# A fused attention and MLP kernel: a third score buffer for the first four pairs, scores of two row blocks as one step, feed-forward chunks of 512 tokens

## The chip, the cores and the metric

One NeuronCore of a Trainium2 chip runs the whole program. The metric is the time of one execution on the device in microseconds. The core's engines are TensorE (PE in the rows; the loads of its weights are PEld), VectorE (DVE), ScalarE (ACT), GpSimd (POOL) and SyncE (SP), which issues the DMAs.

## What is computed

Four sequences of 576 tokens go through three layers. Blockwise causal attention (8 heads of 64 channels, blocks of 64 tokens); then a layer that turns each channel by an angle and mixes the tokens; then a low-rank token mix and a feed-forward of width 2048:

```python
scores = scale * q @ k^T, masked by block, softmax over keys; x = attn @ v
theta = x @ w_theta
zr, zi = x * np.cos(theta), x * np.sin(theta)
u = x + w_tok_r @ zr + w_tok_i @ zi
x = u + np.maximum(u @ w_ch, 0.0)
u = x + (x^T @ U @ V)^T
out = u + np.maximum(u @ w_ch1, 0.0) @ w_ch2
```

## The kernel before, in words

The work is cut into steps, which are recorded and then put in order by a planner inside the program (class `Line`). It keeps a model of each engine, gives each step a due time (`at_time`, `spread`, and the constants `CFG`), and issues on each engine the ready step with the smallest due time for which buffers are free; a few rounds revise the due times. So the order of each engine is fixed when the program is built, and a change of the buffers (`line.home`) or of the steps moves instructions everywhere. On the chip each engine works its list off in that order and waits where an input is late.

**Attention** works on 16 pairs of heads, four per sequence. For a pair, `prep` loads q, k and v, `smax(gp, t)` makes the softmax of row block t (0 to 4): scores on TensorE into a score buffer `s` of two PSUM banks (one half per head), a memset of the masked corner and a maximum on VectorE, and an exponential with its sum on ScalarE. Blocks 0 and 1 share one score buffer, 0 in its first 128 columns, 1 in columns 256 to 511. There are two score buffers (`ss0`, `ss1`). `norm` divides by the sum, `trans` turns the probabilities over by transposes on TensorE (tiles `t`), and `av` multiplies with v (tiles `oA`, `oB`). While one pair is in `trans` and `av`, the next is in `smax`.

**Mixing**, once per sequence: `theta` (th), `sines` on ScalarE, which loads another table for sines than for exponentials, `product` (transposes xp), `mix_r` and `mix_i` (y), `chan` (c), `lowrank` (xq, G) and `expand` (h). The next sequence's attention runs between.

**Feed-forward**: the 2304 tokens are cut into chunks (`CHUNKS`, line 57). For each of 16 slices f of the width, `ff1` makes 12 matmuls into a tile m, ScalarE and VectorE turn m into hh (its rounded part and the rest), and `ff2` makes 12 matmuls into four accumulators acc. A chunk's input u is read back by `load_u` and split in two parts. The first chunk runs beside the last sequence.

PSUM has eight banks: two for `pa` (t, oA, oB, some others, later acc), two for `pm` (th, xp, y, c, xq, h), four for the two score buffers, which later become a3 and b3 of the feed-forward.

**Fillers.** Where the planner's model has TensorE idle in its first 140 us, `keep_warm` puts transposes of the identity into a bank that is free then:

```python
for i in range(int((o.start - end - 60) / 110)):
    w = Op()
    w.call = [(real.tensor.transpose, (v, ident, ident), {})]
```

In the rows a filler stands under the name of that bank's next tile: th<-ident or t<-ident, with ident alone as its input. Since every instruction is issued by one loop, all have that loop's line.

Of the kernel before, what the change touches and what calls it, by code (L numbers as in the profile page):

```python
# [12 lines left out]
F32 = mybir.dt.float32  # L13
F32R = mybir.dt.float32r
# [10 lines left out]
P = 128  # L25
# [28 lines left out]
NHH = 2  # L54
LOC1 = "BBKKXTTTRRRRRRRB"
LOC2 = "BBKKXTTTTTTKKKKB"
CHUNKS = [512] + [256] * 7
NVV = 2
QW = 640
NPT = 1  # L60
# [119 lines left out]
class Line:  # L180
# [33 lines left out]
    def together(self, way):  # L214

        self.choice = []
        way()
        choice, self.choice = self.choice, None
        o = choice[0]
        o.call = [c for x in choice for c in x.call]  # L220
        o.cost = sum(x.cost for x in choice) + (107.0 if o.mode[0] == 64 else 0.0)
        o.outs, o.ins = [a for x in choice for a in x.outs], [a for x in choice for a in x.ins]
        return self.link([o])

# [303 lines left out]
def build(tc, ctx, qT, kT, v, w_theta, wtokT, w_ch, U, V, w1, w2, outT):  # L528
# [21 lines left out]
    def decode(parts, ta, oh, ol):  # L550
# [12 lines left out]
        if ol is not None:  # L563
# [20 lines left out]
    nc = line = Line(nc)  # L584
    pools = {"wk": ctx.enter_context(tc.tile_pool(name="wk", bufs=1)),
             "ps": ctx.enter_context(tc.tile_pool(name="ps", bufs=1, space=PSUM))}
    ast = ExitStack()
    with tc.using_default_side("right"):
        pools["at"] = ast.enter_context(tc.tile_pool(name="at", bufs=1))
        pools["ps2"] = ast.enter_context(tc.tile_pool(name="ps2", bufs=1, space=PSUM))  # L590
# [3 lines left out]
    for pool, tags in (("wk", {"K": 8, "T": NKT, "R": NR, "RT": NT_, "raw": NRAW, "xT": NXT, "Ust": 1, "Vst": 1}),  # L594
                       ("at", FIRST), ("w1p", THEN)):
        for tag, n in tags.items():
            for i in range(n):
                line.home("ps2" if tag == "ss" else pool, f"{tag}{i}", **{tag: tuple(FIRST) if pool == "w1p" else ()})
    for i in range(2):
        line.home("ps3", f"a3{i}", a3=tuple(FIRST))  # L600
        line.home("ps3", f"b3{i}", hp=tuple(FIRST))
        line.home("ps", f"pm{i}", pm=(), hp=("pm",))
    for i in range(PA):
        line.home("ps", f"pa{i}", pa=())

# [21 lines left out]
    def xtile(name, shape, dt):  # L627
        return line.tile(shape, dt, "xT", name)
# [21 lines left out]
    def smax(gp, t):  # L650
# [5 lines left out]
        nm, sm = x["nm"], x["sm"]  # L656
        q, k = qk[gp]
        if t != 1:
            x["s"] = line.tile([P, 2, 512], F32, "ss", f"s{n}_{t}", PSUM)
        s = x["s"]  # L660
        i = 2 * t
        if t < 4:
            W = P * (t + 1)
            src = s[:, :, 256:512] if t == 1 else s[:, :, :W]
            line.together(lambda: [nc.tensor.matmul(src[:, hh], q[64 * hh:64 * hh + 64, t * P:(t + 1) * P],
                                                    k[64 * hh:64 * hh + 64, :W], start=True, stop=True) for hh in range(2)])
            nc.vector.memset(src[0:64, :, W - 64:W], NEG)
            pt = line.tile([P, 2, W], F32, f"P{t}", f"P{n}_{t}")
            nc.vector.tensor_reduce(out=nm[:, i:i + 2], in_=src, axis=AX.X, op=ALU.max, negate=True)
            for hh in range(2):  # L670
# [344 lines left out]
    def load_u(n):  # L1015
        s0, s1 = starts[n], starts[n + 1]
        w = s1 - s0

        def utile(name, shape):
            return line.tile(shape, F32R, "U", name)  # L1020

        if n == 0:
            us[n] = [utile(f"us{n}_{a}", [P, NC4, w]) for a in range(2)]
        else:
            u = utile(f"us{n}", [P, NC4, 2, w]) if n > 1 else xtile(f"us{n}", [P, NC4, 2, w], F32R)
            us[n] = [u[:, :, a] for a in range(2)]
        uh, ul = us[n]
        for c in range(NC4):
            raw = rawslot(f"u3_{n}_{c}", F32)[:, :s1 - s0]
            for b in range(s0 // S, (s1 + S - 1) // S):  # L1030
                a0, a1 = max(s0, b * S), min(s1, (b + 1) * S)
                nc.sync.dma_start(raw[:, a0 - s0:a1 - s0], u3d[b][c * P:(c + 1) * P, a0 - b * S:a1 - b * S])
            rnd("sh", uh[:, c], raw)
            sub(ul[:, c], raw, uh[:, c], "sl")
# [111 lines left out]
    def place(x):  # L1146
        if not isinstance(x, View):
            return x
        buf = x.buf
        if buf.ap is None:  # L1150
            if buf.home.pool not in pools:
                ast.close()
                with tc.using_default_side("right"):
# [54 lines left out]
```

## Time and profile before

| what | us |
|---|---|
| median of 3 runs (902.42 to 905.83) | 902.61 |
| the profiled execution | 902.81 |
| its span, first to last instruction | 901.0 |
| PE busy | 881.4 |
| DVE busy | 420.6 |
| ACT busy | 393.5 |
| POOL busy | 280.8 |

The profile is of one execution. Its span lies 1.8 us under its time. "Busy" counts an engine's instructions as the profile shows them; TensorE's matmuls overlap, and their ends are modelled, so small waits between them hide in it. Matmuls on 32-bit data (s, oA, oB) stand as two records each in the trace, so a step of two such matmuls is x4 there and x2 in the order.

### The profile page before, as it was taken

Reading aid. Unit: us, or ns where it says so; the run is one execution under the profiler, and the core shown is the slowest. Engines: PE = TensorE matmul, PEld = TensorE weight load, DVE = VectorE, ACT = ScalarE, POOL = GpSimd, SP = SyncE. Lnnn points to the kernel's source line nnn. Section 1 sums busy time; section 2 is a strip of 40 time slices with the busy share of each in tenths; the row PEclk is TensorE's granted clock in tenths of the full one; section 3 lists DMA queues with packets and bytes.
Section 4 is the critical chain, followed back from the end, with each engine's and each line's share of the span. In section 5 each row is a group of like instructions: output and inputs, shape, how many; then the busy total and the mean of one; then the engine's idle time right before and its main releaser. Section 6 shows DMA issues by size and latency. Waiting matters only on the chain.

```text
span 901.0 us, 15779 instructions
## 1 busy us (share of the span) xinstructions
PE 881.4 (98%) x6275; PEld 772.0 (86%) x6275; DVE 420.6 (47%) x855; ACT 393.5 (44%) x932; POOL 280.8 (31%) x334
## 2 busy tenths in 40 slices
PE   8999999998999999999999999999999999999998
PEld 7766688876688787898887978899999999999998
DVE  4876687465644566528957782322121212121211
ACT  5977696469644685545735561121111111111111
POOL 2544455554323532346614533221020202020000
PEclk9999999998999999999999999999999999999999
DMA  5551232011020110124343350130010101000000
GB/s 197 171 157 64 70 108 77 29 42 43 29 95 16 43 43 2 68 105 131 104 135 115 111 179 19 49 99 25 1 46 3 43 6 47 3 25 1 25 1 24
DMA packets 45065, 57.39 MB, mean 64 GB/s; under 512 B 5056, under 2 KB 31168, under 8 KB 44992
## 3 DMA queue, kind: packets, MB, share of 16 engines
q1 hardware_dynamic: 44992, 56.39, 19.4%
q8 instruction: 49, 0.80, 0.4%
q14 instruction: 24, 0.20, 0.1%
HBM read 46.94 MB, written 9.44 MB: 63 GB/s over the span
## 4 chain that ended last, share of the span: by engine, by line
PE 82%; DVE 6%; ACT 6%; DMA 2%; issue 2%; POOL 1%; DVEq 0%; POOLq 0%; ACTq 0%; SPq 0%
PE acc L1162 22%; PE m L1162 22%; PE y L1162 11%; PE th L1162 7%; PE t L1162 5%; PE s L1162 5%; PE c L1162 4%; PE oB L1162 3%; DVE d_w L1162 2%; ACT L1162 1%; ACT P L1162 1%; PE G L1162 1%; PE oA L1162 1%; DMA q<-qT 1%; DVE f L1162 1%
## 5 line engine op out<-in xcount | busy, mean ns | idle before, releaser
L1162 PE MATMUL acc<-hh,w 128*128 128x256 f32 (+1 forms) x1440 | 215.7, 297 | 0.3 <-DVE o L1162 0.2
L1162 PE MATMUL m<-us,w 128*128 128x256 f32 (+1 forms) x1440 | 213.5, 296 | 0.4 <-DVE w L1162 0.4
L1162 PEld LDWEIGHTS acc<-hh,w 128*128 128x128 f32 x1440 | 191.0, 190 | 8.3 <-DVE o L1162 0.8
L1162 PEld LDWEIGHTS m<-us,w 128*128 128x128 f32 x1440 | 189.4, 189 | 7.7 <-DVE w L1162 0.8
L1162 ACT ACTIVATE hh<-m 128x256 fp32r<-128x256 f32 (+1 forms) x128 | 52.5, 410 | 300.6 <-PE m L1162 294.2
L1162 DVE SCALAR_TENSOR_TENSOR hh<-m,hh 128x256 fp32r<-128x256 f32 (+1 forms) x128 | 58.5, 457 | 266.9 <-ACT hh L1162 266.8
L1162 PE MATMUL y<-wtok,zh 128*128 128x288 f32 x576 | 122.6, 303 | 0.2
L1162 PEld LDWEIGHTS y<-wtok,zh 128*128 128x128 f32 x576 | 93.8, 190 | 4.0 <-DVE xT L1162 1.1
L1162 ACT ACTIVATE P<-s,nm 128x128 f32<-128x128 f32 (+2 forms) x144 | 78.7, 550 | 40.8 <-DVE nm L1162 40.5
L1162 PE MATMUL y<-wtok,zl 128*128 128x288 f32 x288 | 86.1, 301 | 0.1
L1162 PE MATMUL t<-ident,P 128*128 128x128 f32 x400 | 65.4, 284 | 5.3 <-DVE PTA L1162 2.5
L1162 PE MATMUL s<-k,q 64*128 64x128 f32 (+4 forms) x320 | 68.5, 467 | 1.8 <-ACT P L1162 1.8
L1162 DVE TENSOR_REDUCE nm<-s 128x2 f32<-128x256 f32 (+4 forms) x80 | 63.7, 805 | 2.4 <-PE s L1162 1.2
L1162 PEld LDWEIGHTS t<-ident,P 128*128 128x128 f32 x400 | 47.1, 143 | 20.3 <-issue 5.2
L1162 PE MATMUL c<-u,wch 128*128 128x288 f32 x384 | 59.1, 301 | 0.9 <-DVE u L1162 0.9
L1162 PEld LDWEIGHTS c<-u,wch 128*128 128x128 f32 x384 | 53.6, 188 | 5.1 <-DVE u L1162 1.3
L1162 PEld LDWEIGHTS y<-wtok,zl 128*128 128x128 f32 x288 | 54.4, 189 | 1.9 <-POOL zl L1162 0.6
L1162 PE MATMUL th<-wth,xh 128*128 128x512 f32 x160 | 51.5, 403 | 0.2
L1162 DVE TENSOR_TENSOR xT<-y,xT 128x288 f32<-128x288 f32 x64 | 28.9, 455 | 47.8 <-PE y L1162 47.3
L1162 POOL TENSOR_SCALAR us<-u 128x256 fp32r<-128x256 f32 x5 | 2.4, 480 | 146.7 <-PE m L1162 73.4
L1162 ACT COPY PTB<-t 128x512 f32<-128x512 f32 (+3 forms) x71 | 30.9, 456 | 37.4 <-PE t L1162 36.0
L1162 POOL TENSOR_TENSOR o<-us 128x256 f32<-128x256 f32 x28 | 20.1, 736 | 85.8 <-DMA outT<-o 84.9
(153 smaller groups left out, 1247.1 us busy)
## 6 DMA issues: line engine op xcount, KB each, us to landing
raw_w<-w SPq DMA_DIRECT2D x32, 512.0 KB, 3.8
raw_tok<-wtokT SPq DMA_DIRECT2D x18, 288.0 KB, 3.0
q<-qT SPq DMA_DIRECT2D x16, 320.0 KB, 2.9
vr<-v SPq DMA_DIRECT2D x16, 320.0 KB, 3.2
k<-kT SPq DMA_DIRECT2D x16, 288.0 KB, 3.4
u3d<-xT SPq DMA_DIRECT2D x16, 288.0 KB, 2.2
outT<-o SPq DMA_DIRECT2D x28, 128.0 KB, 1.8
raw_th<-w_theta SPq DMA_DIRECT2D x8, 256.0 KB, 5.1
```

The costliest lines, as they stand in the source:

```text
L1162: fn(*[place(x) for x in args], **{k: place(x) for k, x in kw.items()})
```

## The change

Four edits. The first four pairs get a third score buffer, `ss2`, in the two banks that `pm` takes over afterwards: `pm` is free only when the last of these buffers (tag `s0`) is done with, and its pool `pp` is opened then. The scores of row blocks 0 and 1 are issued as one step of four matmuls, and both masked corners are filled by one memset of a strided view. The chunks of the feed-forward become 512, 256, 512, 512, 512 tokens; chunk 1 takes its u from one buffer of the tag xT, chunk 3 from two of these, the others from the two large buffers U. And the planner's price of a step of several 64-row matmuls is 53.5 ns per matmul more, where it was 107 per step.

```diff
--- before.py
+++ after.py
@@ -54,7 +54,7 @@
 NHH = 2
 LOC1 = "BBKKXTTTRRRRRRRB"
 LOC2 = "BBKKXTTTTTTKKKKB"
-CHUNKS = [512] + [256] * 7
+CHUNKS = [512, 256, 512, 512, 512]
 NVV = 2
 QW = 640
 NPT = 1
@@ -218,7 +218,7 @@
         choice, self.choice = self.choice, None
         o = choice[0]
         o.call = [c for x in choice for c in x.call]
-        o.cost = sum(x.cost for x in choice) + (107.0 if o.mode[0] == 64 else 0.0)
+        o.cost = sum(x.cost for x in choice) + (53.5 * len(choice) if o.mode[0] == 64 else 0.0)
         o.outs, o.ins = [a for x in choice for a in x.outs], [a for x in choice for a in x.ins]
         return self.link([o])
 
@@ -584,7 +584,8 @@
     nc = line = Line(nc)
     pools = {"wk": ctx.enter_context(tc.tile_pool(name="wk", bufs=1)),
              "ps": ctx.enter_context(tc.tile_pool(name="ps", bufs=1, space=PSUM))}
-    ast = ExitStack()
+    ast, pst = ExitStack(), ExitStack()
+    pools["px"] = pst.enter_context(tc.tile_pool(name="px", bufs=1, space=PSUM))
     with tc.using_default_side("right"):
         pools["at"] = ast.enter_context(tc.tile_pool(name="at", bufs=1))
         pools["ps2"] = ast.enter_context(tc.tile_pool(name="ps2", bufs=1, space=PSUM))
@@ -595,11 +596,15 @@
                        ("at", FIRST), ("w1p", THEN)):
         for tag, n in tags.items():
             for i in range(n):
-                line.home("ps2" if tag == "ss" else pool, f"{tag}{i}", **{tag: tuple(FIRST) if pool == "w1p" else ()})
+                if tag == "ss":
+                    line.home("ps2", f"ss{i}", ss=(), s0=())
+                else:
+                    line.home(pool, f"{tag}{i}", **{tag: tuple(FIRST) if pool == "w1p" else ()})
+    line.home("px", "ss2", s0=())
     for i in range(2):
         line.home("ps3", f"a3{i}", a3=tuple(FIRST))
         line.home("ps3", f"b3{i}", hp=tuple(FIRST))
-        line.home("ps", f"pm{i}", pm=(), hp=("pm",))
+        line.home("pp", f"pm{i}", pm=("s0",), hp=("s0", "pm"))
     for i in range(PA):
         line.home("ps", f"pa{i}", pa=())
 
@@ -656,15 +661,22 @@
         nm, sm = x["nm"], x["sm"]
         q, k = qk[gp]
         if t != 1:
-            x["s"] = line.tile([P, 2, 512], F32, "ss", f"s{n}_{t}", PSUM)
+            x["s"] = line.tile([P, 2, 512], F32, "s0" if gp < 4 else "ss", f"s{n}_{t}", PSUM)
         s = x["s"]
         i = 2 * t
         if t < 4:
             W = P * (t + 1)
             src = s[:, :, 256:512] if t == 1 else s[:, :, :W]
-            line.together(lambda: [nc.tensor.matmul(src[:, hh], q[64 * hh:64 * hh + 64, t * P:(t + 1) * P],
-                                                    k[64 * hh:64 * hh + 64, :W], start=True, stop=True) for hh in range(2)])
-            nc.vector.memset(src[0:64, :, W - 64:W], NEG)
+            if t == 0:
+                both = [(s[:, :, :P], 0, P), (s[:, :, 256:512], P, 2 * P)]
+            elif t > 1:
+                both = [(src, t * P, W)]
+            if t != 1:
+                line.together(lambda: [nc.tensor.matmul(y[:, hh], q[64 * hh:64 * hh + 64, c0:c0 + P],
+                                                        k[64 * hh:64 * hh + 64, :w], start=True, stop=True)
+                                       for y, c0, w in both for hh in range(2)])
+                last = s.rearrange("p h (g c) -> p h g c", c=64)[0:64, :, 1::6] if t == 0 else src[0:64, :, W - 64:W]
+                nc.vector.memset(last, NEG)
             pt = line.tile([P, 2, W], F32, f"P{t}", f"P{n}_{t}")
             nc.vector.tensor_reduce(out=nm[:, i:i + 2], in_=src, axis=AX.X, op=ALU.max, negate=True)
             for hh in range(2):
@@ -1019,11 +1031,13 @@
         def utile(name, shape):
             return line.tile(shape, F32R, "U", name)
 
-        if n == 0:
+        if n == 1:
+            u = xtile(f"us{n}", [P, NC4, 2, w], F32R)
+            us[n] = [u[:, :, a] for a in range(2)]
+        elif n % 2:
+            us[n] = [xtile(f"us{n}_{a}", [P, NC4, w], F32R) for a in range(2)]
+        else:
             us[n] = [utile(f"us{n}_{a}", [P, NC4, w]) for a in range(2)]
-        else:
-            u = utile(f"us{n}", [P, NC4, 2, w]) if n > 1 else xtile(f"us{n}", [P, NC4, 2, w], F32R)
-            us[n] = [u[:, :, a] for a in range(2)]
         uh, ul = us[n]
         for c in range(NC4):
             raw = rawslot(f"u3_{n}_{c}", F32)[:, :s1 - s0]
@@ -1148,6 +1162,9 @@
             return x
         buf = x.buf
         if buf.ap is None:
+            if buf.home.pool not in pools and buf.home.pool == "pp":
+                pst.close()
+                pools["pp"] = ctx.enter_context(tc.tile_pool(name="pp", bufs=1, space=PSUM))
             if buf.home.pool not in pools:
                 ast.close()
                 with tc.using_default_side("right"):
```

Since the planner sets the order, the diff does not show what moves. TensorE's list begins, before, with the first pair's scores (s_0_t is row block t of pair 0; 37 fillers precede them):

```order
L1162 MATMUL th_0_112<-ident 128x128 x37
L1162 MATMUL s_0_0_150<-k_0_95,q_0_93 128x128 x2
L1162 MATMUL s_0_2_155<-k_0_95,q_0_93 128x384 x2
L1162 MATMUL th_0_112<-ident 128x128 x10
L1162 MATMUL s_0_0_150<-k_0_95,q_0_93 128x256 x2
L1162 MATMUL th_0_112<-ident 128x128 x25
L1162 MATMUL s_0_3_213<-k_0_95,q_0_93 128x512 x2
L1162 MATMUL th_0_112<-ident 128x128 x15
L1162 MATMUL s_0_4_252<-k_0_95,q_0_93 128x288 x2
L1162 MATMUL th_0_112<-ident 128x128 x16
```

and after the change:

```order
L1179 MATMUL t_0_0_1_115<-ident 128x128 x37
L1179 MATMUL s_0_0_153<-k_0_98,q_0_96 128x128 x2
L1179 MATMUL s_0_0_153<-k_0_98,q_0_96 128x256 x2
L1179 MATMUL s_0_2_160<-k_0_98,q_0_96 128x384 x2
L1179 MATMUL s_0_3_164<-k_0_98,q_0_96 128x512 x2
L1179 MATMUL t_0_0_1_115<-ident 128x128 x22
L1179 MATMUL s_0_4_205<-k_0_98,q_0_96 128x288 x2
L1179 MATMUL t_0_0_1_115<-ident 128x128 x14
L1179 MATMUL s_1_0_246<-k_1_104,q_1_102 128x128 x2
L1179 MATMUL s_1_0_246<-k_1_104,q_1_102 128x256 x2
```

The scores of blocks 0 and 1 now stand together, blocks 2 and 3 follow at once, and the fillers after the first 37 come later. Over the whole program there are 315 fillers before and 180 after; changes between 64-row scores, matmuls of 64 output columns (oA, oB) and full ones are 142 before and 119 after. Ahead of the first sine, ScalarE has 187 instructions before and 190 after, and VectorE, ahead of the first product with a sine, 182 and 203.

ScalarE's list at the sines of the second sequence (f and c are its angles, P a softmax of the third), before:

```order
L1162 ACTIVATE c_3_2478<-c_3_2478,halfpi 128x512
L1162 ACT_TABLE_LOAD
L1162 ACTIVATE P_1_3_2547,sm_1_2383<-s_1_3_2515,nm_1_2371 128x512
L1162 ACT_TABLE_LOAD
L1162 ACTIVATE f_0_2262<-f_0_2262 128x512
L1162 ACT_TABLE_LOAD
L1162 ACTIVATE P_1_3_2547,sm_1_2383<-s_1_3_2515,nm_1_2371 128x512
L1162 ACT_TABLE_LOAD
L1162 ACTIVATE f_1_2283<-f_1_2283 128x512
L1162 ACT_TABLE_LOAD
L1162 ACTIVATE P_1_4_2614,sm_1_2383<-s_1_4_2520,nm_1_2371 128x576
L1162 ACT_TABLE_LOAD
```

and after:

```order
L1179 ACT_TABLE_LOAD
L1179 ACTIVATE f_4_2380<-f_4_2380,tbias,tscale 128x512
L1179 ACTIVATE c_0_2304<-c_0_2304,halfpi 128x512
L1179 ACTIVATE c_1_2316<-c_1_2316,halfpi 128x512
L1179 ACTIVATE c_2_2384<-c_2_2384,halfpi 128x512
L1179 ACTIVATE c_3_2391<-c_3_2391,halfpi 128x512
L1179 ACTIVATE f_0_2138<-f_0_2138 128x512
L1179 ACTIVATE f_1_2168<-f_1_2168 128x512
L1179 ACTIVATE f_2_2253<-f_2_2253 128x512
L1179 ACTIVATE f_3_2302<-f_3_2302 128x512
L1179 COPY PTB_1_2489<-t_1_2_0_2479 128x3x128
```

The sines now stand together; the program holds 14 table loads before and 8 after.

TensorE's list ahead of the first sequence's mixing (y; xp are transposes for the products), before:

```order
L1162 MATMUL oB_1_1397<-PTB_1_1333,vr_1_1047 64x64 x2
L1162 MATMUL s_2_3_1421<-k_2_1015,q_2_1011 128x512 x2
L1162 MATMUL xp_4_1432<-ident,xd_1257 128x128 x4
L1162 MATMUL t_2_0_1_1450<-ident 128x128 x25
L1162 MATMUL xp_1_1476<-ident,xT_440 128x128 x4
L1162 MATMUL t_2_0_1_1450<-ident 128x128 x26
L1162 MATMUL xp_2_1528<-ident,xT_440 128x128 x4
L1162 MATMUL xp_3_1535<-ident,xT_440 128x128 x4
L1162 MATMUL t_2_0_1_1450<-ident 128x128 x7
L1162 MATMUL y_0_0_0_1556<-wtok_480,zh_8_1481 128x288 x2
```

and after:

```order
L1179 MATMUL oB_2_1443<-PTB_2_1393,vr_2_1089 64x64 x2
L1179 MATMUL xp_1_1465<-ident,xT_440 128x128 x4
L1179 MATMUL t_3_0_0_1488<-ident 128x128 x18
L1179 MATMUL xp_2_1507<-ident,xT_440 128x128 x4
L1179 MATMUL xp_3_1516<-ident,xT_440 128x128 x4
L1179 MATMUL t_3_0_1_1530<-ident 128x128 x7
L1179 MATMUL y_0_0_0_1538<-wtok_564,zh_8_1451 128x288 x2
```

Two of three blocks of fillers are gone or shorter, and before the excerpt now stand the transposes and value products of one more pair of the second sequence, the third instead of the second (oB_2 where it was oB_1).

## Rows read from the trace of the kernel before

**Rows 1.** The page, part 1: busy time and share of the span, by engine.
```profile
PE 881.4 (98%) x6275; PEld 772.0 (86%) x6275; DVE 420.6 (47%) x855; ACT 393.5 (44%) x932; POOL 280.8 (31%) x334
```

**Rows 2.** Stretches: length; busy us (instructions) of PE, PEld, DVE, ACT, POOL; clock, DMA, GB/s.
```profile
8.90:78.10 69.20, 66.96 (x501) 48.44 (x500) 53.94 (x120) 58.43 (x173) 28.56 (x33) 1.00 0.47 152
78.10:117.40 39.30, 38.60 (x248) 27.16 (x247) 24.64 (x54) 28.45 (x74) 16.65 (x22) 1.00 0.21 67
124.50:180.50 56.00, 54.13 (x396) 47.71 (x396) 37.36 (x80) 34.22 (x90) 30.30 (x36) 0.97 0.21 66
180.50:229.20 48.70, 44.19 (x248) 32.75 (x246) 28.95 (x59) 39.50 (x79) 23.12 (x31) 0.93 0.13 40
294.60:338.00 43.40, 42.27 (x270) 33.87 (x268) 25.93 (x57) 31.38 (x69) 20.77 (x27) 1.00 0.14 43
```

**Rows 3.** Chain of waits, 0 to 125 us: start, length, what.
```profile
1.36 6.28 PE th L1162 x37
...
51.10 3.65 DMA q<-qT
...
119.69 2.84 PE t L1162 x26
```

**Rows 4.** Timeline of PE, first softmax: start, length, instruction, [idle before, releaser].
```profile
11.03 0.70 PE L1162 MATMUL s<-k,q 64*128 64x256 f32 x4 [1.08 <-ACT P L1162]
```

**Rows 5.** Chain of waits, 0 to 125 us: scores and value products.
```profile
20.18 0.42 PE s L1162 x4
...
22.18 0.84 PE s L1162 x4
...
82.59 1.07 PE s L1162 x8
...
89.59 0.80 PE oA L1162 x8
90.39 2.05 PE oB L1162 x20
```

**Rows 6.** Timeline of ACT, sines of the second sequence.
```profile
207.33 1.28 ACT L1162 ACT_TABLE_LOAD   x1
...
209.35 2.55 ACT L1162 ACTIVATE c<-c,halfpi 128x512 f32<-128x512 f32 x4
211.91 1.28 ACT L1162 ACT_TABLE_LOAD   x1
```

**Rows 7.** Timeline of PE in the same stretch.
```profile
220.83 1.08 PE L1162 MATMUL xp<-ident,xT 128*128 128x128 f32 x4 [2.27 <-DVE f L1162]
```

**Rows 8.** Stretches around the falls of the clock, columns as in rows 2.
```profile
0.00:5.55 5.55, 4.19 (x20) 4.19 (x21) 0.29 (x6) 0.00 (x0) 1.42 (x7) 1.00 0.60 178
142.00:145.50 3.50, 3.50 (x18) 3.47 (x18) 2.16 (x6) 1.95 (x5) 1.27 (x1) 0.51 0.40 102
220.50:227.40 6.90, 5.99 (x21) 3.68 (x21) 2.65 (x8) 6.84 (x10) 4.67 (x8) 0.51 0.00 0
```

**Rows 9.** Chain of waits: groups of the first chunk, and one place in two chunks of 256.
```profile
535.93 2.80 PE m L1162 x12
538.73 2.80 PE acc L1162 x12
...
621.53 2.86 PE acc L1162 x24
...
667.06 2.86 PE acc L1162 x24
```

**Rows 10.** Groups by line and form (VectorE's additions), and DMA issues of outT.
```profile
L1162 DVE TENSOR_TENSOR o<-acc,o 128x256 f32<-128x256 f32 x28 | 10.5, 425 | 5.8 <-PE acc L1162 5.8
...
L1162 DVE TENSOR_TENSOR o<-acc,o 128x512 f32<-128x512 f32 x4 | 2.7, 682 | 0.0
...
outT<-o SPq DMA_DIRECT2D x4, 256.0 KB, 2.0
...
outT<-o SPq DMA_DIRECT2D x4, 128.0 KB, 1.8
```

## The prediction

> **What bounds the kernel now.** I read the page's busy times first, then the stretches between the marks of the program, then the chain of waits and the timelines. The reader is to see in the page that TensorE is busy for 881.4 of 901.0 us [rows 1]: whatever shortens this kernel has to take work or waits off TensorE. But busy is not useful here: some of it is filler transposes that write nothing anyone reads. Ahead of the first mixing matmul, at 124.5 us, the order has 314 of them, 277 beyond the first 37, which wait for the first load anyway. The first two stretches [rows 2], up to the first sine, have VectorE at 53.94 and 24.64 us and ScalarE at 58.43 and 28.45 us out of 69.20 and 39.30, so neither of these is full, and the fillers stand where TensorE would wait for them.
>
> **Fillers.** 26 of them take 2.84 us in the chain, 0.109 us each [rows 3]. Counted over the order, the program holds 315 before and 180 after. 135 fewer at 0.109 are 14.7 us of TensorE's queue. They are no gain by themselves: each one goes because a real instruction is there to issue earlier, and where that one is late, the engine waits in the filler's place. What releases work earlier can be seen in the first softmax [rows 4]: the scores of row block 1 share their buffer with those of block 0 and wait 1.08 us, until ScalarE has read those; with both issued as one step that wait is gone, and with a third buffer the next pair's scores start before this pair's are read. Whether the helpers can follow is the question. Ahead of the first sine the order puts 203 VectorE instructions instead of 182 (more of the next pairs' softmax) and 190 on ScalarE instead of 187. VectorE's mean in the two stretches is 78.6 us over 174 instructions, 0.45 us, so it gets 9.5 us more, about 88; ScalarE three more at some 0.5, about 88.3 instead of 86.9 [rows 2]. From 8.9 us on, both are then busy until 97 us at the least, and the first sine is at 117.4 now. So it comes from 20 us earlier to not at all. The loads move along on SP's queue: q, k and v have two buffers each, so a pair's load still stands behind the scores of two pairs before, and the chain has a wait of 3.65 us for q [rows 3], which earlier scores can only move. I take that TensorE keeps the share it has now, because the fillers of before filled their gaps with little left over (2.24 us idle in 69.20), which says that the waits are about as long as the order assumes. I charge 1.5 us for busier helpers and the loads; the ends are 0 and, if no filler's time comes back, the first rival. The banks of the third buffer come free with the last scores of the fourth pair; by the order the first theta matmul stands some 30 rows behind those, so nothing waits there. The joint memset of blocks 0 and 1 saves VectorE 16 small ones: nothing, since it isn't full.
>
> **Changes of matmul shape.** A visit to the 64-row scores costs more than its columns: block 0 alone takes 0.42 us, block 2 alone 0.84, both in a row 1.07 [rows 5]. Going there and back thus costs 0.19 us, 0.095 a change. By the order there are 142 changes between the three shapes (64 rows, 64 columns, full) before and 119 after: 23 at 0.095 are 2.2 us.
>
> **The sines of the second sequence.** ScalarE's timeline shows table loads of 1.28 us, and sines and exponentials in turn between them [rows 6]; the program has 14 in all. After the change it has 8, one at the start and two per sequence, less one at the end: the nine sine instructions of a sequence then stand together. From 180.5 to 229.2 us TensorE waits 2.27 us in one piece for f [rows 7], and is idle for 48.70 - 44.19 = 4.51 us in all [rows 2]; and its clock is at 0.51, close to the lower of its two levels, from 220.5 to 227.4 us, right behind this wait [rows 8], which wastes half of 6.90, 3.4 us. Together 7.9. The same stretch of the third sequence, which has no such loads, is still idle for 43.40 - 42.27 = 1.1 us [rows 2]. I take 6.5 us; the ends are 0, if the stall only changes its place, and 7.9. What is late next there is the exponential behind the block of sines (four of them take 2.55 us), and TensorE has the mixing of the first sequence to do meanwhile.
>
> **Feed-forward.** Seven chunks of 256 and one of 512 tokens become one of 256 and four of 512. A steady chunk of 256 takes 667.06 - 621.53 = 45.53 us, the distance of the same place in two chunks; a group of twelve 512-column matmuls takes 2.80, so 32 groups take 89.6 [rows 9]. Three times 2 x 45.53 - 89.6 = 1.46 gives 4.4 us. ScalarE's and VectorE's part of a group lies beside TensorE's, as it does in the 512 chunk now, whose groups follow each other every 2.80 us. At a hand-over VectorE has to empty four accumulators, 4 x 0.68 us [rows 10], while TensorE has two groups of the next chunk to do, 5.6 us: nothing; without that cover 2.7 us each time. A 512 chunk's u needs both large buffers, which come free when the chunk two before has ended, and the chunk between gives the loads 45 or 90 us: nothing. The output of the last chunk is larger: the last addition takes 0.68 instead of 0.42 us and the landing 2.0 instead of 1.8 [rows 10]: 0.5 us more, all of it at the end.
>
> **Sum.** -14.7 - 2.2 - 6.5 - 4.4 + 1.5 + 0.5 = -25.8 us. The profiled execution took 902.81 us, 0.2 above the median of the three, 902.61, so I count from either: 877.
>
> **The clock, and a rule on it.** Before 5.55 us TensorE did nothing but fillers; 20 of them took 4.19 us, 0.21 each, twice the 0.109 of later [rows 3, 8] (the 1.00 that the view prints there is not borne out by them). So such transposes alone brought the clock from the lower level to the upper. Taking 135 of them away can therefore have a price. The rows bound it: where the clock fell, it stayed at 0.51 for 3.5 or 6.9 us [rows 8], at a loss of 1.7 to 3.4 us. I take none, since where fillers go, real matmuls stand closer; the other end is the second rival. The Trainium skill ("TensorE: Matmul & The Clock Gate", Part 4 on transposes) says that the full clock does not engage for transposes, which don't count as a busy engine in the same way. By that rule the fillers never held the clock, and taking them away could not lower it: the sum would be the same 877 and the second rival would fall. The rows here speak against the rule.
>
> **Rivals.** *The helpers are full* (0.2). If ScalarE keeps the 80% it has now (86.9 of 108.5 us), its 88.3 us take 110.4, until 119.3 us: the first sine comes no earlier, and waits take the fillers' place. What is left is the work done ahead by then: by the order one more pair's 25 transposes (2.7 us), its value products (0.80 and 2.05) and the scores of blocks 0 to 2 of the pair behind (0.42, 0.70 and 0.84) [rows 4, 5]. That is 7.5, with 6.5 for the sines and 4.4 - 0.5 for the feed-forward: 885. For it: ScalarE is the fullest of the two now. Against it: it waits in between for maxima that come from TensorE's scores. *The clock falls in the first sequence* (0.03). Thinner fillers leave gaps, each is followed by a drop. A drop costs 1.7 to 3.4 us and the wait ahead of it some 1.5 to 2.3 [rows 7]: some 4.5 us each. Six would eat the 25.8 us; eight in 120 us, one a softmax, give 913, slower than before. Against it: between 8.9 and 124.5 us there is not one now [rows 2]. *More of the waits go* (0.15). Idle time of 2.24 + 0.70 + 1.87 us in the first 180 [rows 2] and the drop at 142 us (1.75) [rows 8] would also go, and the 1.5 that I charged: 869. *The new chunks don't run as the first* (0.02): the hand-over without cover costs 4 x 2.7 = 11 us more: 888.
>
> **Numbers.** The forecast (faster, order of waits as now) has 0.6, with 871 to 884 of its own from the ends of the sine term and of the helpers' charge; 877 is its middle. The range of 868 to 889 takes in the full helpers and the vanished waits with the same play, and leaves out the falling clock and the edges. A measurement of this kernel can tell some 0.5%, 4.5 us, from no change. Faster by more than that: 0.6 + 0.2 + 0.15 and a little of the rest, 0.95; the same 0.03; slower 0.02.
>
> **What would show it.** First mixing matmul near 118 us instead of 124.5 (14.7 and a little less for fillers and changes of shape, 1.5 more for the helpers, and 7.5 of work done ahead), with some 5 us idle before it; 8 table loads; no low clock near 220 us; chunks of 512 tokens every 89.6 us; the last addition 0.68 us. It is wrong if the first mixing comes after 123 us, if a table load stands between two sines, or if TensorE waits at a hand-over.

## The result and the profile after

The changed kernel takes 876.52 us in the median (874.64 to 882.76, 4 runs), the kernel before 902.51 beside it: a ratio of 0.972, interval 0.969 to 0.975. The profiled execution took 876.27 us, its span is 874.5. The forecast of 877.0 was met; how it was met is another matter.

The page's busy times of the changed kernel, which answer to [rows 1]:

```profile
PE 851.5 (97%) x4988; PEld 697.2 (80%) x4988; DVE 434.7 (50%) x814; ACT 378.1 (43%) x868; POOL 241.1 (28%) x273
```

TensorE is busy for 29.9 us less and still fills 97% of the span: the time went off its list. Where, the starts of four matmuls show (us from the span's start, from the timelines):

| mark | before | after | stretch before | stretch after |
|---|---|---|---|---|
| first mixing matmul y | 124.5 | 125.2 | 124.5 | 125.2 |
| first G, sequence 1 | 229.2 | 209.1 | 104.7 | 83.9 |
| first h of the last sequence | 581.6 | 561.3 | 352.4 | 352.2 |
| end | 901.0 | 874.5 | 319.4 | 313.2 |

So nothing was gained ahead of the first mixing (+0.7), 20.8 us between it and the first G, 0.2 from there to the last expansion, and 6.2 in the feed-forward behind it: 26.5 in all.

Stretches of the changed kernel, columns as in [rows 2]; the first two end where theta and the sines of sequence 1 begin, as there:

```profile
8.90:73.10 64.20, 59.46 (x433) 39.77 (x429) 54.87 (x123) 56.86 (x170) 27.70 (x35) 1.00 0.52 167
73.10:116.00 42.90, 40.07 (x246) 27.75 (x244) 32.31 (x73) 32.75 (x86) 15.83 (x22) 1.00 0.23 74
125.20:169.30 44.10, 43.59 (x310) 37.91 (x311) 34.88 (x74) 32.21 (x84) 20.76 (x21) 1.00 0.26 77
169.30:209.10 39.80, 39.80 (x260) 32.84 (x258) 24.11 (x49) 26.33 (x57) 17.67 (x24) 1.00 0.11 32
```

Ahead of the first sine TensorE now idles 4.74 + 2.83 us, where it was 2.24 + 0.70 [rows 2]. Behind the first mixing it idles 0.5 us, where it was 1.87 + 4.51, and the low clock of 3.4 and 6.8 us [rows 8], which wastes half of itself, 5.1, is gone. So 11.0 of the 20.8 us are stalls that vanished; the other 9.8 are work that no longer stands in this stretch. Most of it is done ahead, where TensorE had fillers before: between the two marks the trace has 26 records of t, 12 of s, 8 of oA and 20 of oB fewer, and ahead of the first mixing 25, 16, 8 and 20 more. Four xp and four xq have only moved behind the first G.

The stretch up to the first mixing matmul as a whole, before and after, columns as in [rows 2]:

```profile
0.00:124.54 124.54, 120.02 (x848) 88.57 (x849) 85.64 (x194) 94.01 (x260) 52.10 (x66) 1.00 0.39 128
```
```profile
0.00:125.16 125.16, 114.93 (x783) 80.95 (x784) 96.48 (x216) 98.39 (x274) 49.71 (x68) 1.00 0.42 135
```

TensorE is busy there for 5.1 us less and idle for 5.7 us more. What it waits for is in its waits up to the first mixing matmul (us in total, times, longest), after:

```profile
PE t L1179 <- DVE PTB L1179: 2.4, 4, 0.8
PE s L1179 <- ACT P L1179: 1.7, 3, 0.8
...
PE xp L1179 <- DVE f L1179: 1.2, 2, 0.9
PE t L1179 <- ACT PTB L1179: 1.1, 3, 0.4
```

and three rows of the same view before, where all five add up to 4.1 us, against 9.7 in ten rows after:

```profile
PE s L1162 <- ACT P L1162: 1.3, 2, 1.1
PE t L1162 <- ACT PTA L1162: 0.6, 1, 0.6
PE t L1162 <- ACT P L1162: 0.5, 2, 0.3
```

The transposes t now wait for the copies that empty their two banks (PTB), and xp waits for VectorE's products. The wait for ScalarE's P, which the joint step was to remove [rows 4], is no shorter: it has moved from row block 1 to the scores of block 4.

ScalarE's timeline at the sines of sequence 2, which answers to [rows 6]:

```profile
199.15 1.28 ACT L1179 ACT_TABLE_LOAD   x1
200.44 0.82 ACT L1179 ACTIVATE f<-f,tbias,tscale 128x512 f32<-128x512 f32 x1
201.16 2.54 ACT L1179 ACTIVATE c<-c,halfpi 128x512 f32<-128x512 f32 x4
203.61 2.18 ACT L1179 ACTIVATE f<-f 128x512 f32<-128x512 f32 x4
```

All nine sines are done 6.6 us after the table load starts. TensorE's waits in 125.2 to 209.1 us are two rows, where [rows 7] alone had 2.27:

```profile
PE t L1179 <- ACT P L1179: 0.3, 1, 0.3
PE c L1179 <- DVE xT L1179: 0.2, 1, 0.2
```

In the chain of waits, the chunks of 512 follow each other without a wait ([rows 9] had 45.53 us for half as many tokens):

```profile
692.44 5.60 PE m L1179 x24
698.04 2.76 PE acc L1179 x12
700.80 2.75 PE m L1179 x12
...
781.22 5.44 PE m L1179 x24
...
870.45 0.69 DVE o L1179
```

From 692.44 to 781.22 are 88.8 us, from 603.1, where the chunk before begins, 89.3; the last addition takes 0.69 [rows 10].

### The profile page after: what moved, and what is told of

Its sections match the earlier page's. It is cut to its first block, busy times and chain, and to the rows that moved or that the text cites. A ratio compares the mean times of both kernels' runs of the same rounds, so it can differ in the third digit from the quotient of the medians.

```text
span 874.5 us, 12850 instructions
## 1 busy us (share of the span) xinstructions
PE 851.5 (97%) x4988; PEld 697.2 (80%) x4988; DVE 434.7 (50%) x814; ACT 378.1 (43%) x868; POOL 241.1 (28%) x273
## 4 chain that ended last, share of the span: by engine, by line
PE 48%; DVE 3%; DMA 1%; ACT 1%; issue 1%; ACTq 0%; DVEq 0%; SPq 0%
PE acc L1179 22%; PE m L1179 21%; PE y L1179 3%; PE c L1179 1%; DMA raw_w<-w 1%; DVE d_w L1179 1%; DVE o L1179 1%; ACT d_w L1179 1%; PE G L1179 0%; DVE xT L1179 0%; ACT raw_w L1179 0%; PE xq L1179 0%; PE h L1179 0%; DVE w L1179 0%; DVE zl L1179 0%
## 5 line engine op out<-in xcount | busy, mean ns | idle before, releaser
L1179 PE MATMUL acc<-hh,w 128*128 128x512 f32 (+1 forms) x900 | 205.1, 373 | 1.9 <-DVE hh L1179 1.4
L1179 PE MATMUL m<-us,w 128*128 128x512 f32 (+1 forms) x900 | 202.9, 372 | 0.0
L1179 PEld LDWEIGHTS acc<-hh,w 128*128 128x128 f32 x900 | 157.1, 188 | 35.1 <-DVE hh L1179 2.3
L1179 DVE SCALAR_TENSOR_TENSOR hh<-m,hh 128x512 fp32r<-128x512 f32 (+1 forms) x80 | 50.9, 636 | 264.9 <-ACT hh L1179 264.8
L1179 PEld LDWEIGHTS m<-us,w 128*128 128x128 f32 x900 | 156.6, 188 | 30.2
L1179 ACT ACTIVATE hh<-m 128x512 fp32r<-128x512 f32 (+1 forms) x80 | 44.4, 555 | 292.7 <-PE m L1179 287.6
L1179 PE MATMUL s<-k,q 64*128 64x128 f32 (+4 forms) x320 | 65.2, 452 | 1.8 <-ACT P L1179 1.7
L1179 POOL TENSOR_TENSOR o<-us,us 128x512 f32<-128x512 f32 x16 | 22.0, 1404 | 125.0 <-DVE o L1179 84.2
L1179 ACT COPY PTB<-t 128x384 f32<-128x384 f32 (+3 forms) x66 | 29.4, 454 | 33.2 <-PE t L1179 32.0
L1179 ACT ACTIVATE P<-P,rs 128x128 f32<-128x128 f32 (+4 forms) x72 | 38.4, 592 | 4.1 <-DVE rs L1179 4.1
```

Source lines behind the costliest of these rows:

```text
L1179: fn(*[place(x) for x in args], **{k: place(x) for k, x in kw.items()})
```

## The experiments

Twelve kernels, in the order of the questions. "Later" and "earlier" compare profiled executions, times are medians; the kernel before took 902.9 to 903.8 us beside them. The marks are those of one execution each, and they scatter: up to the last sequence e_chunks has TensorE's list of the kernel before and e_attn that of the changed kernel, and their first mixing comes 1.0 us later and 1.9 us earlier than there. A difference of marks under 2 us shows nothing by itself. The times of the changed kernel scatter over 8 us. The marks of all kernels, in us:

| kernel | time | first mixing | first G | between | fillers | table loads |
|---|---|---|---|---|---|---|
| before | 902.5 | 124.5 | 229.2 | 104.7 | 315 | 14 |
| after | 876.5 | 125.2 | 209.1 | 83.9 | 180 | 8 |
| e_chunks | 897.1 | 125.6 | 230.6 | 105.0 | 315 | 14 |
| e_attn | 881.1 | 123.3 | 207.5 | 84.2 | 180 | 8 |
| e_twobuf | 884.9 | 129.4 | 216.0 | 86.6 | 217 | 8 |
| e_nojoint | 894.3 | 121.1 | 222.1 | 101.0 | 257 | 16 |
| e_sines | 901.3 | 124.4 | 226.6 | 102.2 | 315 | 8 |
| e_loads | 886.0 | 125.0 | 215.6 | 90.6 | 180 | 14 |
| e_nofill_after | 880.8 | 126.7 | 211.6 | 84.9 | 0 | 8 |
| e_nofill_before | 905.6 | 126.9 | 230.7 | 103.8 | 0 | 14 |
| e_pe | 880.9 | 129.3 | 213.7 | 84.4 | 257 | 8 |
| e_act | 879.6 | 126.2 | 210.2 | 84.0 | 180 | 8 |
| e_dve | 881.8 | 129.2 | 212.9 | 83.7 | 180 | 8 |
| e_eps | 875.6 | 122.8 | 206.5 | 83.7 | 180 | 8 |

### Which part of the change is worth what

**e_chunks**: the kernel before with the new chunks alone.

```diff
-CHUNKS = [512] + [256] * 7
+CHUNKS = [512, 256, 512, 512, 512]
...
+        if n == 1:
+            u = xtile(f"us{n}", [P, NC4, 2, w], F32R)
...
```

> The kernel before with the new chunks (512, 256, 512, 512, 512) alone; TensorE's list is the same as before up to the end of the last sequence. Theory A (a 512-column group costs 2.80 us against two of 1.423 of 256 columns): 902.5 - 4.4 + 0.5 = 898.6. Rival B (the feed-forward stretch of the changed kernel was 6.2 us shorter than before, and all of that is due to the chunks): 896.3. Between them lies the fall of the clock at 582 us, which before has and the changed kernel has not: if this run has it too, A.

Measured: 897.05 us, ratio 0.993 (0.991 to 0.996), 6.3 us: between A and B, nearer B. The fall of the clock at 582 us isn't in this profile. From the start of the third chunk (the second of 256, or of 512) to the end it takes 270.9 us, where the kernel before takes 276.8; the clock stayed up in this stretch in both while TensorE worked.

**e_attn**: the changed kernel with the old chunks, the same edit undone.

> The changed kernel with the old chunks (512 and seven of 256); third buffer and joint step stay, TensorE's list is the changed kernel's up to the end of the last sequence. Theory A: the chunks are worth 4 us also here, so 876.5 + 4 = 880.5, and the attention part alone gives 22 us of the 26. Rival B: with the old chunks the hand-overs or the loads of u disturb the last sequence, and the two parts don't add up: over 884.

Measured: 881.07 us, ratio 0.977 (0.975 to 0.979). The attention part alone gives some 22 us; 4.6 of the 26 are missing, the feed-forward's. The same stretch to the end takes 276.8 us here and 271.4 in the changed kernel. Theory A holds: the two halves of the change add up within what the medians tell apart (22.3 + 6.3, against 26.0 to 27.3).

**e_twobuf**: the changed kernel without the third buffer.

```diff
-    line.home("px", "ss2", s0=())
```

> The changed kernel without the third score buffer; joint step and new chunks stay. Its order has 217 fillers (180 in the changed kernel, 315 before) and 8 table loads. Theory A (before the first mixing ScalarE and VectorE set the time, so what TensorE could start earlier is worth little there): 876 to 880, with the first mixing at 124 to 128 us. Rival B (the prediction's own account: 37 more fillers are 37 x 0.109 = 4.0 us of TensorE's queue): 880.5. Rival C (the third buffer is what brings most of the gain): over 888.

Measured: 884.89 us, ratio 0.980 (0.978 to 0.983), 8.4 us over the changed kernel by the medians, 7.9 by the spans, between what B and C expected. 4.2 us come ahead of the first mixing matmul, 2.7 between it and the first G.

**e_nojoint**: the changed kernel without the joint step.

```diff
-            if t == 0:
-                both = [(s[:, :, :P], 0, P), (s[:, :, 256:512], P, 2 * P)]
...
+            line.together(lambda: [nc.tensor.matmul(src[:, hh], q[64 * hh:64 * hh + 64, t * P:(t + 1) * P],
+                                                    k[64 * hh:64 * hh + 64, :W], start=True, stop=True) for hh in range(2)])
+            nc.vector.memset(src[0:64, :, W - 64:W], NEG)
```

> The changed kernel with the scores of row blocks 0 and 1 again as two steps with a memset each; the third buffer and the new chunks stay. Its order has 257 fillers and 16 table loads. Theory A (the joint step is what makes the stalls between the first mixing matmul and the second sequence's go, 15.2 us before and 3.2 after): from the first mixing to the first G 100 us or more instead of 83.9, the whole 888 to 896. Theory B (the third buffer does it): 876 to 880. Theory C (the joint step is worth its changes of shape alone): 879 to 881. The kernel with the joint step and the chunks but two buffers took 884.9.

Measured: 894.30 us, ratio 0.991 (0.987 to 0.994): theory A. The first mixing is even 4.1 us earlier than in the changed kernel (2.2 earlier than in e_attn), and all of that and more is lost behind it. Its stretch from 173.1 to the first G, columns as in [rows 2], and the longest wait there:

```profile
173.10:222.10 49.00, 43.19 (x244) 32.04 (x242) 29.16 (x61) 38.62 (x76) 20.62 (x28) 0.93 0.13 40
```
```profile
214.59 1.65 PE L1172 MATMUL s<-k,q 64*128 64x384 f32 x4 [3.69 <-ACT P L1172]
```

This is the stretch of the kernel before once more (44.19 of 48.70, clock 0.93 [rows 2]), with the wait on another tile. Take the chunks' 6.3 from the gains and the third buffer alone has given 3.2 us and the joint step alone 12; together they give 22. The planner's new price differs from the old one only for a step of four matmuls (214 ns instead of 107), so it counts with the joint step here; no run tries it alone. The joint step also changes the order of the sines (8 table loads instead of 16), so the next two kernels look at those alone. No run puts the sines of e_nojoint itself together.

### The sines

**e_sines**: the kernel before, with the last four sines of sequence 2 moved ahead of the three exponentials between them.

```diff
-    order = line.plan(ROUNDS)
+    order = hoist(line.plan(ROUNDS))
```

`hoist` moves, in ScalarE's list alone, every sine of a sequence that stands behind an exponential between its sines to the place ahead of that exponential.

> The kernel before, with one thing changed: in ScalarE's list the four sines f_0 to f_3 of the second sequence stand ahead of the three exponentials that came between them, so that 8 table loads are left of 14. The other engines' lists, the fillers, the score buffers and the chunks are those of before. Theory A (the interleaved sines cost what the stretch from 180.5 to 229.2 us lost): the 2.27 us wait of TensorE for f and the low clock from 220.5 to 227.4 us go, 6.5 to 8 us less: 894.5 to 896. Rival B (the stall changes its place: the exponentials are late instead, and TensorE waits for them): 901 to 903. If A holds, then most of what the change gained between 125 and 229 us has nothing to do with the third buffer or the joint step by themselves, only with the order that came out.

Measured: 901.26 us, ratio 0.998 (0.997 to 1.000), 1.3 us (0 to 2.8 by the interval) where 6.5 to 8 were expected: theory A falls, B holds. TensorE's waits from 179 to 240 us:

```profile
PE xp L1183 <- DVE f L1183: 1.6, 1, 1.6
PE t L1183 <- POOL P L1183: 1.3, 2, 1.0
```

and the stretch of the low clock, which was 6.9 us long in [rows 8]:

```profile
219.60:233.30 13.70, 11.28 (x43) 7.83 (x42) 6.80 (x15) 4.75 (x12) 6.00 (x10) 0.50 0.00 1
```

The wait for f is 0.7 shorter, the transposes of the exponentials that now come later wait instead, and the clock stays low for twice as long. That this order keeps it low is not shown: e_chunks, with the list of the kernel before, has 13.7 us there too. The first G is 2.6 us earlier, the next mixing matmul not at all (236.3 against 236.1).

**e_loads**: the other way round. The changed kernel gets its table loads back.

```diff
+            if i in second[5:8]:
+                w = Op()
+                w.call = [(real.scalar.activation, (), dict(out=scratch, in_=ident, func=AF.Exp))]
+                out.append(w)
```

> The changed kernel with three exponentials of 128x128 added between the last four sines of the second sequence, whose results nobody reads: 14 table loads instead of 8, as in the kernel before, six of 1.28 us and three small exponentials, some 8.7 us on ScalarE between 203.6 and 205.8 us of the changed kernel. Theory A (the prediction's sine term: what the loads delay, TensorE waits for): the last sine ends near 214.5 instead of 205.8, the xp that now waits 0.92 us for f at 211.74 waits several us more, a low clock may follow; the whole 5 to 8 us longer, 881.5 to 884.5. Theory B (TensorE has the mixing of the first sequence to do meanwhile, and the loads alone cost little, as in the kernel before, where taking them out gave 1.3): within 2 us of 876.5.

Measured: 885.97 us, ratio 0.981 (0.978 to 0.984), 9.5 us over the changed kernel (8.2 by the spans, 7.7 by the ratios): theory A, 1.5 us above its range. ScalarE's timeline and TensorE's waits from 200 to 222 us:

```profile
204.04 1.28 ACT L1192 ACT_TABLE_LOAD   x1
205.33 0.31 ACT L1192 ACTIVATE scratch<-ident 128x128 f32<-128x128 f32 x1
205.66 1.28 ACT L1192 ACT_TABLE_LOAD   x1
206.96 0.63 ACT L1192 ACTIVATE f<-f 128x512 f32<-128x512 f32 x1
...
214.06 0.63 ACT L1192 ACTIVATE f<-f 128x512 f32<-128x512 f32 x1
214.59 0.46 ACT L1192 COPY PTB<-t 128x384 f32<-128x384 f32 x1
214.95 0.59 ACT L1192 CAST x2h<-xq 128x512 fp32r<-128x512 f32 x1
```
```profile
PE G L1192 <- ACT x2h L1192: 6.6, 1, 6.6
```

Not the sines themselves are waited for, but x2h, which stands behind them on ScalarE's list. Behind this wait the clock fell, as the expectation allowed:

```profile
213.80:220.60 6.80, 4.60 (x17) 3.69 (x18) 4.27 (x10) 4.69 (x11) 1.89 (x2) 0.50 0.01 2
```

In this order some 8 us are on the path, the low clock included. So the loads are worth 7.7 to 9.5 us here, and taking them out of the other order was worth 1.3: the term belongs to an order, not to the loads.

### What sets the first mixing matmul

**e_nofill_after** and **e_nofill_before**: no fillers, all else in the same order.

```diff
-WARM = 140e3
+WARM = 0.0
```

> The changed kernel without any filler transpose, all else in the same order (876.5 us with them; 180 fillers at 0.109 us, of which 37 stand ahead of the first load). Theory A (ahead of the first mixing matmul the helpers set the pace and a filler only fills a wait): first mixing matmul at 125 us as now, within 2 us, and the whole 876.5 within 2 us; the rows of waits grow by some 15 us in the first 125. Theory B (the fillers hold the clock): the granted clock falls behind the waits, each fall 3.4 to 6.9 us long at a loss of 1.7 to 3.4; six or more of them in the first 125 us, 887 to 900 us. Theory C (fillers cost TensorE's queue): 143 fillers at 0.109 come back, first mixing at 110, the whole near 861. By the rule of the Trainium skill (TensorE: Matmul & The Clock Gate, Part 4) that transposes do not engage the full clock, no fall would be new and the time be that of A.

> The kernel before without any filler transpose, all else in the same order (903.4 us with them; 315 fillers, 278 of them behind the first load, 30.3 us of TensorE's queue). Theory A (a filler only fills a wait): first mixing matmul within 3 us of 124.5, the whole 901 to 905. Theory B (fillers hold the clock): falls in the first 125 us, where there is none now; with twice the fillers of the changed kernel more of them than there: 915 to 930. Theory C (fillers cost the queue): up to 30 us less, 873.

Measured: 880.82 us, ratio 0.976 (0.972 to 0.980), and 905.59, ratio 1.003 (1.001 to 1.005). First mixing 1.5 and 2.4 us later, though 15.6 and 30.3 us of fillers are gone: C falls, and A holds for the marks; the times are 2 us above A's in the first and at its edge in the second. TensorE's waits up to there in the changed kernel without fillers add up to 24.2 us, 14.5 more than with them:

```profile
PE s L1179 <- ACT P L1179: 9.1, 6, 2.4
PE s L1179 <- POOL q L1179: 4.6, 1, 4.6
```

The falls of B are there too, four of them, 24.0 us of low clock in the first 121 (columns as in [rows 2]):

```profile
11.50:25.20 13.70, 10.02 (x29) 4.91 (x28) 9.39 (x22) 12.66 (x41) 6.57 (x9) 0.50 0.47 144
...
49.00:52.50 3.50, 3.03 (x11) 2.39 (x12) 3.10 (x7) 3.04 (x9) 2.43 (x4) 0.51 0.39 118
...
62.70:66.10 3.40, 3.17 (x9) 1.48 (x10) 2.14 (x5) 2.31 (x6) 1.82 (x3) 0.50 0.56 174
...
117.30:120.70 3.40, 3.30 (x18) 1.90 (x18) 3.40 (x8) 3.39 (x7) 0.91 (x1) 0.50 0.24 73
```

They would cost up to 12 us if TensorE's list were what counts there, and the mark shows 1.5, within its scatter. The two effects, waits in the fillers' place and a slower clock, aren't separated by this pair.

**e_pe**: half as many fillers again behind the first 9 us, 77 more.

```diff
-                    for i in range(int((o.start - end - 60) / 110)):
+                    for i in range(int((o.start - end - 60) / 110 * (1.0 if o.start < 9e3 else 1.5))):
```

> The changed kernel with half as many fillers again behind the first 9 us: 257 instead of 180, 77 more at 0.109 us, 8.4 us of TensorE's queue ahead of the first mixing matmul. Theory A (TensorE's queue is not what sets the first mixing, its waits take up the fillers, as taking 143 away gained nothing): first mixing matmul within 2 us of 125.2, the whole 876 to 879. Theory B (the order assumed the waits about as long as they are, as the prediction took it): first mixing at 133, the whole 884 to 886.

Measured: 880.88 us, ratio 0.976 (0.974 to 0.978). The first mixing comes 4.1 us later, between A and B: half of the 8.4 us are paid. TensorE's waits are only 2.0 us shorter than in the changed kernel (7.7 in all).

**e_act** and **e_dve**: idle instructions on ScalarE (24) and VectorE (30), spread over their lists ahead of the first mixing.

```diff
+                w.call = [(real.scalar.activation, (), dict(out=scratch, in_=ident, func=AF.Copy))]
...
+                w.call = [(real.vector.tensor_tensor, (), dict(out=scratch, in0=ident, in1=ident, op=ALU.add))]
```

> The changed kernel with 24 copies of 128x128 on ScalarE added, spread between its 10th instruction and the first sine; nobody reads them. At the 0.25 to 0.34 us of the smallest ScalarE rows that is 6 to 8 us. Theory A (ScalarE sets when the first mixing starts): first sine and first mixing matmul 5 to 8 us later, 130 to 133, the whole 881 to 885. Theory B (TensorE's own queue sets it, as the prediction took it): the copies lie in ScalarE's idle time, first mixing at 125 to 127, the whole 876 to 878. Theory C (VectorE sets it, ScalarE waits for VectorE): as B, with ScalarE's idle time smaller.

> The changed kernel with 30 additions of 128x128 on VectorE added, spread between its 10th instruction and the first that uses xp; nobody reads them. At some 0.2 us each that is 6 us. Theory A (ScalarE sets when the first mixing starts, VectorE waits for it): first mixing matmul at 125 to 127, the whole 876 to 878. Theory B (TensorE's queue sets it): the same. Theory C (VectorE sets it): first mixing 5 to 7 us later, 130 to 132, the whole 881 to 884.

What was added, by groups of instructions up to 125 us, in the two kernels:

```profile
L1193 ACT ACTIVATE scratch<-ident 128x128 f32<-128x128 f32 x24 | 7.5, 314 | 0.0
```
```profile
L1193 DVE TENSOR_TENSOR scratch<-ident 128x128 f32<-128x128 f32 x30 | 11.8, 392 | 0.0
```

Measured: 879.62 us, ratio 0.974 (0.970 to 0.978), first mixing 1.0 us later; and 881.77 us, ratio 0.976 (0.973 to 0.980), 4.0 us later. For ScalarE, A falls: the mark is as B or C has it, the time 1.6 us above theirs. For VectorE the time is in C's range, the mark a little short of it; the additions took twice the expected 6 us. Of ScalarE's added work 1.0 of 7.5 us shows, which the scatter of the marks covers; of VectorE's a third, of TensorE's (e_pe) half. None of the three shows in full, so none of these engines alone sets the first mixing. That the path goes from one to the other is a reading of this and not shown.

**e_eps**: an attempt at a version that beats both. Each sum of a softmax is at least 1, so adding 1e-9 to it changes nothing in 32 bits. The addition is left out, and the reciprocal reads the sum.

```diff
+                if kw.get("scalar1") == 1e-9:
+                    eps[id(kw["out"].buf)] = kw["in0"]
+                    continue
```

> The changed kernel in its own order, with the addition of 1e-9 to the 16 sums of the softmax left out (the reciprocal reads the sums themselves; each sum is at least 1). 16 VectorE instructions of 0.29 us fewer, 7 of them ahead of the first mixing matmul, 2.1 us. Theory A (VectorE's work there costs a third of its length, as 11.8 us more cost 4.0): first mixing some 0.7 us earlier, the whole 875 to 876.5, not to be told from the changed kernel by the time alone. Theory B (the reciprocal stands in the chain of each softmax, and each pair gains 0.3 us on the path): 872 to 874. Theory C (VectorE waits anyway): 876.5.

Measured: 875.64 us, ratio 0.970 (0.968 to 0.971). The first mixing comes 2.4 us earlier and the first G 2.6, but only 0.5 and 1.0 earlier than in e_attn, so A's 0.7 is neither met nor refuted; at the end 0.4 is left, 0.9 in the medians. The intervals of this kernel and the changed one overlap: it isn't told apart from it.

## Why the prediction was right, point by point

**Fillers and helpers (-14.7 + 1.5): wrong.** The step that failed is "I take that TensorE keeps the share it has now". TensorE's list up to the first mixing did lose 134 fillers, 14.6 us, for some 7 us of real work, but the mark stood at 125.2 us, not 118 (123.3 in e_attn, with the same list), and by the prediction's own test, 123, this part was wrong. TensorE's busy time up to there fell by only 5.1 us, since the work done ahead took more than its 7.5, and waits grew by 5.7, 5.6 of it in the waits above. The helpers' work came as summed: up to the first sine VectorE was busy for 87.2 us and ScalarE for 89.6, where 88 and 88.3 were forecast. The prediction had read the fillers' number as the length of the waits; with all fillers gone the mark hardly moves, with more it moves by half. What was gained of this term is the work done ahead, 7.5 by the rival's count.

**The rival "the helpers are full": its mark held, its reason did not.** The first sine came at 116.0 us, 1.4 earlier, and the waits took the fillers' place, as it said. But ScalarE, which it took to be the full one, is not: 7.5 us more on it cost 1.0. Its 885 missed by 8.5 us because it carried the other terms at the prediction's sizes and left the changes of shape out.

**Sines (-6.5): the mark right, the size too small, the cause wider.** 8 table loads, no low clock near 220 us, as forecast. In the stretch that this term was read from, the stalls of 7.9 us (4.51 and the low clock's 3.4) went whole, its upper end. Another 3.1 went ahead of it, which the prediction had left to the rival of the waits that go: 11.0 in all from the first mixing to the first G, not 6.5. e_sines shows that standing the sines together is not enough: alone it gives 1.3. e_loads shows that in the new order they are necessary: their separation costs 7.7 to 9.5, the low clock that follows included. What else the order does there, above all that the softmax of the following pairs is further ahead, so that nothing waits for the exponentials behind the sines, was only argued; e_nojoint, with the third buffer but without the joint step, has the stall, and e_twobuf, with the joint step and two buffers, has not (86.6 us between the marks). So the joint step, its price and the order that comes with them do this, and the third buffer alone does not; what in the order does it stays open.

**Changes of shape (-2.2): not measured alone.** No run isolates them. They, the work done ahead and the four xp and four xq behind the mark are the 9.8 us by which TensorE's work between the two marks shrank; 7.5 and 2.2 would make 9.7, which proves neither.

**Feed-forward (-4.4, and +0.5 at the end): right in kind, too small.** Predicted -3.9, measured -5.4 (changed kernel against e_attn, to the end) to -5.9 (e_chunks against before). The mis-sized number is the chunk of 512: 88.8 to 89.3 us instead of 89.6, since half of the groups in it take 2.75 us, not 2.80. Three pairs of chunks at 91.06 less about 89.1 are 5.9, less 0.5 for the tail 5.4. No hand-over waits. The 6.2 us from the last expansion on hold some 0.8 more, because the clock fell near 582 us before and at that place not at all in the changed kernel: with the new chunks this stretch took 312.7 to 313.2 us in the four kernels without such a fall, and 313.3 to 314.0 in the six that have one.

**The clock.** In the profile no fall cost the changed kernel anything, as taken. The second rival needed eight falls in 120 us; e_nofill_after has four there with no filler at all and ends 4.3 us later, with an interval that overlaps the changed kernel's.

**The sum.** -25.8 was forecast, -26.5 came by the spans. Two errors cancelled: 7.2 us that did not come ahead of the first mixing, and about as much that came behind it (-20.8 where work done ahead and sines made 14) and in the feed-forward (1.5 to 2 more). That 877 was met to half a microsecond is luck; that the stalls at the sines and the feed-forward would shrink, and where, is not.

## What to carry to other kernels

A filler, or any instruction put where a planner's model sees idle time, tells how long the model thinks the wait is, not how long it is. Before counting removed fillers as gain, take them all out once: if the engine's next milestone doesn't move, the waits behind them are what has to be shortened. Read the granted clock of that run too, since here it fell with the fillers gone.

A cost measured in one order of instructions (here the separate sines) can't be carried into another. Ask what stands behind the delayed instruction on its engine in the new order; six table loads cost 7.7 to 9.5 us in one order here and 1.3 in the other.

## What the runs showed of the hardware

**The clock and fillers.** With fillers the granted clock reached its upper level, 2.4 GHz, at 4.2 to 6.9 us in the twelve kernels that have them, and in the profile of the changed kernel it stayed there until 873.9. Without them it first rose at 8.1 and 23.2 us, and then was at the lower level, 1.2 GHz (0.50 to 0.51 in the rows), for 24.0 us of the first 121 in the one kernel and at 36.8, 105.1 and 122.2 us in the other. The Trainium skill ("TensorE: Matmul & The Clock Gate", Part 4 on transposes) would have it that transposes do not engage the full clock; these runs speak against it, as the rows before did: in the kernel before and the changed one the clock rose at 5.6 and 6.9 us, when TensorE had done fillers alone (its first other matmul starts at 7.57 and 8.25).

**The same list, other falls.** e_chunks has TensorE's list of the kernel before up to the feed-forward and waits in the same place, but its clock was low from 221.0 for 13.7 us, where it was 6.8 before, and the first G came 1.4 us later, 1.0 of which it was late already at the first mixing. The profile of the changed kernel has no fall in its body; e_attn, e_act, e_dve and e_eps, on its list or nearly, each have one at 113 to 118 us and one at 561 to 565, and e_eps a third at 455. The mean granted clock of the changed kernel's other three executions was 0.994 to 0.998, where the profiled one had 1.000. A fall of 3.4 us seen in one profile is thus no fixed cost of a kernel.

**A table load.** In e_loads the next instruction starts 1.29 us after the load's start, and six loads with three exponentials of 0.31 delayed the last sine by 9.1 us. The Trainium skill ("ScalarE: Activation LUTs", What ACT_TABLE_LOAD costs) gives 1283 ns for the load, which the trace shows, and some 1380 ns of drain on top, which it does not.

**Two-input additions on VectorE.** The 128x128 additions of e_dve took 0.392 us in the mean: 23 of the 30 took 0.22 to 0.28, and three took 1.16 to 1.36. What held those up was not tried.
